# adaLN transformer block: chunk 0's high parts straight from the transposes, the first query weights split on GpSimd

## The chip, the core and the metric

The kernel runs on one core of a Trainium2 chip. The engines of a core run side by side, each through its own queue in order: TensorE (PE, and PEld for its weight loads), VectorE (DVE), ScalarE (ACT), GpSimd (POOL) and SyncE (SP, which issues most DMAs). They wait for each other through semaphores. The metric is the time of one execution in microseconds (us), as the median of several runs.

## The reference

One transformer block whose two layer norms are modulated by a condition `c`; 2048 rows of 512 values, 32 heads of 16, a hidden width of 1792, all in float32.

```python
mod = (_silu(c) @ w_mod).reshape(c.shape[0], 6, 1, -1)
sa, ca, ga, sb, cb, gb = (mod[:, 0], mod[:, 1], mod[:, 2], mod[:, 3], mod[:, 4], mod[:, 5])
h = _layernorm(x, axis=-1) * (1 + ca) + sa
x = x + ga * _A_ref(h, A_wqkv, A_wo)      # qkv projection, softmax attention, output projection
h = _layernorm(x, axis=-1) * (1 + cb) + sb
x = x + gb * _B_ref(h, B_w_gate, B_w_up, B_w_down)   # (silu(h @ w_gate) * (h @ w_up)) @ w_down
```

## The kernel before

The rows are worked on in four chunks of 512. Matrix products run in a split form: an operand is written as a high part (rounded to the type fp32r) and a low part (the value less its high part), and a product takes three matmuls: high by high, high by low, low by high. So every operand needs two results: `hT[0]` and `hT[1]` for the modulated, transposed rows of a chunk, `wqs[0]` and `wqs[1]` for the weights of the projections.

The order on each engine is the order in which the code is written out (a manual schedule). A tile framework puts in the semaphore waits, tile by tile.

The change lies in the start-up, before the projections of chunk 0 run without a pause. There the following happens, in this order:

- SP loads the rows `xt`, then for each half `ab` of the 512 features the condition's weights `wm_ab` and, behind each, 128 columns of the projection weights: the first 128 key columns (`wst0[:, 0]`) and the first 128 query columns (`wst0[:, 1]`).
- VectorE computes the statistics of the rows (`stats`) and normalizes them (`norm`, tiles `nt`).
- `mod_part` multiplies the condition by half of `w_mod` on TensorE (L286) into PSUM bank 7 and copies the result to `ev` on ScalarE (L289). `mod_col` turns `ev` on TensorE (L295), sums the pieces on VectorE (`cs`, L297) and writes the columns `modc` of scale and bias (L300).
- `turn` transposes the normalized rows on TensorE (L165), one PSUM bank for each of the four blocks k of 128 features (`tps0`, banks 0 to 3).
- `half_prep(ab)` modulates the two blocks k = 2ab and 2ab+1 into the float32 tile `h32`: the first on VectorE (L172), the second, with `fast`, on ScalarE (L170). ScalarE then rounds each `h32` to its high part (L350), and VectorE subtracts for the low part (L353). The first call stands before the projections, the second behind the third of their matmuls.
- The key columns are split by `split_w`: the high part by ScalarE (L205), the low part by GpSimd (L206). The query columns: the high part by ScalarE (L360), the low part by VectorE (L353), at the head of the subtractions of `half_prep(1)`.

The first job of the projections is `both` of key block 0 and query block 0. Its 24 matmuls (L213) stand in an order by halves of the features: six of the key job for k = 0 and 1 (high by high, low weights, low rows), six of the query job for k = 0 and 1 (high by high, low rows, low weights), then the same two groups of six for k = 2 and 3. The other projections follow without a gap. The transposes of chunk 0 and all that comes later (the other chunks, scores and softmax, the feed-forward layers) are not touched by the change.

Of the kernel before, what the change touches and what calls it, by code (L numbers as in the profile page):

```python
# [11 lines left out]
F32 = mybir.dt.float32  # L12
F32R = mybir.dt.float32r
BF = mybir.dt.bfloat16
I32 = mybir.dt.int32
AF = mybir.ActivationFunctionType
ALU = mybir.AluOpType
# [4 lines left out]
P = 128  # L22
# [6 lines left out]
NK = D // P  # L29
NC = 4  # L30
CW = S // NC
# [25 lines left out]
def run(it):  # L57
    for _ in it:
        pass
# [44 lines left out]
def block_kernel(ctx, tc, x, wqkv, wo, w_gate, w_up, w_down, c, w_mod, out):  # L104
    nc = tc.nc
# [18 lines left out]
    four, bank, single = Turn(0, 1, 2, 3), Turn(4, 5, 6), Turn(7)  # L124
# [18 lines left out]
    def stats(pool, xt, keep):  # L143
        st = pool.tile([P, 4, 6], F32, name="stt", tag="stt", bufs=2)
        mv = pool.tile([P, 4, 2], F32, name="mv", tag="mv", bufs=2)
        rs = pool.tile([P, 4], F32, name="rs", tag="rs", bufs=2)
        for i in range(4):
            nc.vector.bn_stats(st[:, i, :], xt[:, i, :])
            nc.vector.bn_aggr(mv[:, i, :], st[:, i, :])
            yield  # L150
        nc.scalar.activation(rs, mv[:, :, 1], AF.Sqrt, bias=eps_t[:, 0:1])
        keep += [mv, rs]
# [10 lines left out]
    def turn(tp, rows, k):  # L163
        for i, nt in enumerate(rows):
            nc.tensor.transpose(tp[:, i * P:(i + 1) * P], nt[:, k * P:(k + 1) * P], ident)  # L165

    def modulate(pool, hT, tp, vec, k, fast=False, copy=True):
        h32 = pool.tile([P, CW], F32, name="h32", tag="h32", bufs=2)
        if fast:
            nc.scalar.activation(h32, tp, AF.Identity, scale=modc[:, vec, k:k + 1], bias=modc[:, vec + 1, k:k + 1])  # L170
        else:
            nc.vector.tensor_scalar(h32, tp, modc[:, vec, k:k + 1], modc[:, vec + 1, k:k + 1],  # L172
                                    op0=ALU.mult, op1=ALU.add)
        if copy:
            nc.scalar.copy(hT[0][:, k, :], h32)
        return hT[1][:, k, :], h32, hT[0][:, k, :].bitcast(F32)

    def prep(pool, xt, hT, vec, lat):
# [76 lines left out]
    wm_ab = []  # L255
# [27 lines left out]
    def mod_part(wm, copy=nc.scalar.copy):  # L283
        pb_ = single("pmod")
        for k in range(NK):
            nc.tensor.matmul(pb_[32 * k:32 * k + 32, :], sc[:, k:k + 1].to_broadcast([P, 32]), wm[:, k, :],  # L286
                             start=True, stop=True)
        ev = pa.tile([P, D], F32, name="ev", tag="ev", bufs=1)
        copy(ev, pb_)  # L289
        return ev  # L290
# [28 lines left out]
    def split_w(src, c0, eng=nc.gpsimd):  # L319
        cols = slice(c0, c0 + P)  # L320
        split(wqs[0][:, :, cols], wqs[1][:, :, cols], src, eng)
# [4 lines left out]
    hT = {0: new_hT()}  # L326
    keep0 = []
    run(stats(pa, xt[0], keep0))
    split_w(wst0[:, 0], D)
    ev = mod_part(wm_ab[0])  # L330
    rows0 = list(norm(pa, xt[0], keep0))

    def half_cols(ab):
# [1 line left out]

    tps0 = []

    def turn_two(k):
        for e in range(2):
            tps0.append(four("tp"))  # L340
            turn(tps0[-1], rows0, k + e)

    def half_prep(ab, ev, extra=None):
        mod_col(ev, half_cols(ab))
        if ab == 0:
            turn_two(2)
        tps = tps0[2 * ab:2 * ab + 2]
        lows = [modulate(pa, hT[0], tps[e], 0, 2 * ab + e, e, False) for e in range(2)]
        for _, h32, high in lows:
            nc.scalar.copy(high.bitcast(F32R), h32)  # L350
        nxt = mod_part(wm_ab[1]) if ab == 0 else None
        for low in ([extra] if extra else []) + lows:
            nc.vector.tensor_sub(*low)  # L353
        return nxt

    bank = Turn(4, 5, 6, 7)
    turn_two(0)
    ev = half_prep(0, ev)
    wq0 = [w[:, :, 0:P] for w in wqs]
    nc.scalar.copy(wq0[0], wst0[:, 1])  # L360

    def weights():
        st_ = {}
# [94 lines left out]
    for ci in range(NC - 1):  # L458
        jobs = [proj_T(ci, w, m, 1 if ci or m else 2) for w, m in kq[:6 if ci == NC - 2 else 8]]
        if ci < NC - 2:  # L460
            jobs += [proj_v(4 * ci + t) for t in range(4)]
        hT[ci + 1] = new_hT()
        if ci == 0:
            jobs[0:2] = [both(*jobs[0:2], 6)]
        if ci == 1:
            bank = Turn(4, 5, 6)
            sm.add("m", 7, mods())
        if ci:
            sm.add("p", 5 if ci < NC - 2 else 3, prep(pa, xt[ci + 1], hT[ci + 1], 0, 1))
        for i, _ in enumerate(sm.jobs(jobs)):  # L470
            if ci == 0 and i == 2:
                half_prep(1, ev, (wq0[1], wst0[:, 1], wq0[0].bitcast(F32)))
            if ci == 0 and i == 5:
                take(weights_, 2)
                sm.add("w", 5, weights_)
            if ci == 0 and i == 24:
                sm.add("p", 5, prep(pa, xt[1], hT[1], 0, 1))
            if i == 40:
                load_k0(ci)
            if i == 44 and ci + 2 < NC:  # L480
                load_x(ci + 2)
        while sm.lanes["p"][1]:
            run(sm.lanes["p"][1].pop(0))
# [706 lines left out]
```

## Time and profile before

| | us |
|---|---|
| median of 3 runs | 1826.32 (1826.1 to 1827.04) |
| the profiled execution | 1826.86 |
| its span (first to last instruction) | 1825.0 |
| busy: PE / PEld / DVE / ACT / POOL | 1816.3 / 1202.5 / 1521.2 / 1248.0 / 459.9 |

The span is what the trace covers; the profiled execution's own time is 1.86 us longer. TensorE is busy nearly all of the span, at the full granted clock. A busy TensorE is not one at its peak, since its matmuls are pipelined: it shows as busy also where another engine sets its pace. What sets the end is read from the chain of waits, followed back from the last instruction.

### The profile page before, as it was taken

The numbers are of one execution on the slowest core, as the hardware profiler recorded it, in microseconds if no ns is written. First come the engines' busy times: TensorE is split into PE (matmuls) and PEld (weight loads), VectorE is DVE, ScalarE is ACT, GpSimd is POOL, SyncE is SP. The second block draws the span as 40 slices with busy tenths as digits, with TensorE's granted clock in tenths as the row PEclk, the third lists the DMA queues.
The fourth block names the chain that finished last, engine by engine and source line by source line (L and its number), as shares of the span: only waits on it lengthen the run. The fifth ranks groups of instructions, "written<-read, shape, count | busy, mean of one in ns | idle before, by whom it ended". The sixth has DMA issues, their size and how long they took to land.

```text
span 1825.0 us, 40961 instructions
## 1 busy us (share of the span) xinstructions
PE 1816.3 (100%) x16904; PEld 1202.5 (66%) x16904; DVE 1521.2 (83%) x2554; ACT 1248.0 (68%) x2358; POOL 459.9 (25%) x538
## 2 busy tenths in 40 slices
PE   9999999999999999999999999999999999999999
PEld 7876444444465777776565777776564577777887
DVE  5578999999999888888999888889999988832544
ACT  4223888888888766777888767767888876673211
POOL 3612544556223111111123111111113011131200
PEclk9999999999999999999999999999999999999999
DMA  9883876667845444453544554444643536333742
GB/s 307 288 232 138 203 199 172 179 167 199 207 81 125 103 122 143 115 149 70 145 110 105 141 125 118 122 118 91 161 80 57 116 90 157 134 123 120 279 167 108
DMA packets 80486, 267.62 MB, mean 147 GB/s; under 512 B 19604, under 2 KB 24212, under 8 KB 59620
## 3 DMA queue, kind: packets, MB, share of 16 engines
q1 hardware_dynamic: 61324, 179.71, 34.0%
q0 software_dynamic: 18288, 84.49, 19.5%
q8 instruction: 133, 2.18, 0.5%
q10 hardware_dynamic: 688, 0.80, 0.1%
q14 instruction: 53, 0.43, 0.1%
HBM read 201.85 MB, written 62.13 MB: 145 GB/s over the span
## 4 chain that ended last, share of the span: by engine, by line
PE 83%; DVE 14%; ACT 1%; DMA 0%; issue 0%; SPq 0%; DVEq 0%
PE bank L586 21%; PE bank L789 20%; PE bank L571 14%; DVE mx L525 14%; PE bank L523 11%; PE bank L808 8%; PE bank L213 7%; PE bank L851 1%; PE bank L772 0%; DMA wm_ab<-in_w_mod 0%; PE bank L165 0%; ACT sq L832 0%; DVE v_flat L882 0%; PE bank L537 0%; SPq L261 0%
## 5 line engine op out<-in xcount | busy, mean ns | idle before, releaser
L525 DVE TENSOR_REDUCE mx<-bank 128x1 f32<-128x512 f32 x2048 | 1273.3, 681 | 111.0 <-PE bank L523 63.7
L571 PE MATMUL bank<-qop,kop 50*128 50x512 f32 x2048 | 729.7, 426 | 0.4 <-ACT pt__16494 L573 0.2
L523 PE MATMUL bank<-kop,qop 48*128 48x512 f32 x2048 | 724.6, 425 | 0.3
L571 PEld LDWEIGHTS bank<-qop,kop 50*128 50x128 f32 x2048 | 343.1, 184 | 168.9 <-issue 49.8
L523 PEld LDWEIGHTS bank<-kop,qop 48*128 48x128 f32 x2048 | 342.8, 184 | 106.2 <-DVE mx L525 62.1
L789 PE MATMUL bank<-act,wgu 64*128 64x512 f32 x1872 | 303.5, 392 | 0.0
L789 PEld LDWEIGHTS bank<-act,wgu 64*128 64x128 f32 x1872 | 199.4, 187 | 22.5
L613 POOL TENSOR_TENSOR on<-o,rb 128x512 f32<-128x512 f32 x31 | 39.9, 1286 | 507.8 <-DMA rb<-d_dr 359.0
L789 PE MATMUL bank<-wd,mid 64*128 64x512 f32 x912 | 131.6, 391 | 0.0
L870 POOL CAST mid<-m 128x512 fp32r<-128x512 f32 x40 | 24.4, 609 | 380.5 <-DVE m L868 273.7
L789 PEld LDWEIGHTS bank<-wd,mid 64*128 64x128 f32 x912 | 92.2, 186 | 11.2
L213 PE MATMUL bank<-hT,wqs 128*128 128x512 f32 x384 | 94.4, 397 | 0.4 <-DVE wqs L353 0.4
L866 DVE SCALAR_TENSOR_TENSOR q<-th,bank 128x512 f32<-128x512 f32 x56 | 38.3, 683 | 54.2 <-ACT th L862 54.2
L213 PEld LDWEIGHTS bank<-hT,wqs 128*128 128x128 f32 x384 | 70.6, 188 | 19.1 <-issue 3.2
L862 ACT ACTIVATE th<-bank 128x512 f32<-128x512 f32 x56 | 33.2, 594 | 57.9 <-PE bank L808 57.9
L882 DVE TENSOR_TENSOR x<-bank,x 128x512 f32<-128x512 f32 x84 | 53.9, 685 | 16.1 <-PE bank L789 16.1
L868 DVE TENSOR_TENSOR m<-bank,q 128x512 f32<-128x512 f32 x56 | 38.7, 692 | 21.7 <-PE bank L808 19.7
L871 POOL TENSOR_TENSOR mid<-m,mid 128x512 fp32r<-128x512 f32 x40 | 51.7, 1292 | 3.3
L808 PE MATMUL bank<-wd,mid 128*128 128x512 f32 x216 | 51.3, 393 | 0.0
L213 PE MATMUL bank<-wqs,hT 128*128 128x512 f32 x192 | 48.0, 398 | 0.0
L789 PE MATMUL bank<-wgu,act 64*128 64x512 f32 x288 | 47.6, 392 | 0.0
L808 PEld LDWEIGHTS bank<-wd,mid 128*128 128x128 f32 x216 | 40.4, 188 | 8.9
(6300 smaller groups left out, 5137.3 us busy)
## 6 DMA issues: line engine op xcount, KB each, us to landing
wgu<-gu_dr SPq DMA_DIRECT2D x48, 1024.0 KB
wd<-wd_dr SPq DMA_DIRECT2D x28, 1024.0 KB
kop<-kd SPq DMA_DIRECT2D x33, 768.0 KB
kop<-kd POOLq DMA_DIRECT2D x29, 768.0 KB, 8.8
gu_dr<-wgu POOLq DMA_DIRECT2D x14, 1024.0 KB, 13.6
kd<-prt SPq DMA_DIRECT2D x16, 512.0 KB
qd<-prt SPq DMA_DIRECT2D x16, 512.0 KB
kop<-gu_dr SPq DMA_DIRECT2D x8, 1024.0 KB
```

The source lines that it names most:

```text
L213: nc.tensor.matmul(pt, lhs(a, k), rhs(b, k), start=(n == 0), stop=(n == 3 * nk - 1))
L523: nc.tensor.matmul(pm, qop[u][rows, s, qt * P:(qt + 1) * P], kop[u % 3][rows, s, kc * CW:(kc + 1) * CW], start=True, stop=True)
L525: nc.vector.tensor_reduce(mx[u][:, b, s, qt, kc:kc + 1], pm, op=ALU.max, axis=AX.X)
L571: nc.tensor.matmul(sp, kop[u % 3][rows, h // 2, kt * P:(kt + 1) * P], qop[u][rows, h // 2, :], start=True, stop=True)
L586: nc.tensor.matmul(pv[u][32 * h:32 * h + 32, cols], v_flat[:, e0:e0 + 32], p_[h][:, cols], start=(kt == 0 and half == 0), stop=(kt == 15), ...
L613: mul.tensor_mul(on, o, rb)
L789: mm = nc.tensor.matmul(outs[e], lhs(e, a, k)[rows], rhs(b, k)[rows], start=(ph == 0 and j == 0), stop=(j == z and (ph == 1 or trade)), sk ...
L808: nc.tensor.matmul(outs[e], lhs(e, a, k), rhs(b, k), start=(j == 0), stop=(j == z))
L866: nc.vector.scalar_tensor_tensor(q, th, 1.0, outs[0], op0=ALU.add, op1=ALU.mult)
L868: nc.vector.tensor_mul(m32, outs[1], q)
L871: (nc.gpsimd if slow else nc.vector).tensor_sub(mid[:, 1, :], m32, mid[:, 0, :].bitcast(F32))
L882: nc.vector.tensor_add(ch.x2[:, t, :], outs[e], ch.x2[:, t, :])
```

## The change

- `half_prep` no longer calls `modulate` (which loses its options `fast` and `copy`). For each block k ScalarE computes the modulated rows from the transposes' bank directly into the high part `hT[0]`, and VectorE computes the same from the same bank into `h32`; then VectorE subtracts for the low part.
- The first query columns are split on GpSimd: it rounds the high part and subtracts for the low part. ScalarE's cast and VectorE's subtraction for them go.
- The copy of the first `ev` stands before the cast of the first key columns on ScalarE.
- Only one block of rows is transposed before `ev` is turned, the other three behind it.

```diff
     run(stats(pa, xt[0], keep0))
+    ev = mod_part(wm_ab[0])
     split_w(wst0[:, 0], D)
-    ev = mod_part(wm_ab[0])
...
-    def half_prep(ab, ev, extra=None):
+    def turn_next():
+        tps0.append(four("tp"))
+        turn(tps0[-1], rows0, len(tps0) - 1)
+
+    def half_prep(ab, ev):
         mod_col(ev, half_cols(ab))
-        if ab == 0:
-            turn_two(2)
-        tps = tps0[2 * ab:2 * ab + 2]
-        lows = [modulate(pa, hT[0], tps[e], 0, 2 * ab + e, e, False) for e in range(2)]
-        for _, h32, high in lows:
-            nc.scalar.copy(high.bitcast(F32R), h32)
+        while len(tps0) < NK:
+            turn_next()
+        lows = []
+        for k in (2 * ab, 2 * ab + 1):
+            scale, bias = modc[:, 0, k:k + 1], modc[:, 1, k:k + 1]
+            h32 = pa.tile([P, CW], F32, name="h32", tag="h32", bufs=2)
+            nc.scalar.activation(hT[0][0][:, k, :], tps0[k], AF.Identity, scale=scale, bias=bias)
+            nc.vector.tensor_scalar(h32, tps0[k], scale, bias, op0=ALU.mult, op1=ALU.add)
+            lows.append((hT[0][1][:, k, :], h32, hT[0][0][:, k, :].bitcast(F32)))
         nxt = mod_part(wm_ab[1]) if ab == 0 else None
-        for low in ([extra] if extra else []) + lows:
+        for low in lows:
             nc.vector.tensor_sub(*low)
         return nxt
...
-    turn_two(0)
+    turn_next()
     ev = half_prep(0, ev)
     wq0 = [w[:, :, 0:P] for w in wqs]
-    nc.scalar.copy(wq0[0], wst0[:, 1])
+    nc.gpsimd.tensor_copy(wq0[0], wst0[:, 1])
+    nc.gpsimd.tensor_sub(wq0[1], wst0[:, 1], wq0[0].bitcast(F32))
...
-                half_prep(1, ev, (wq0[1], wst0[:, 1], wq0[0].bitcast(F32)))
+                half_prep(1, ev)
```

VectorE's queue from the first sum of the condition's columns to the last low part of chunk 0, with the engine whose semaphore each row waits for. First the kernel before (`h_204` and `h_242` are VectorE's blocks 0 and 2; banks 63 to 66 are banks 0 to 3, bank 70 is bank 7):

```order
L297 TENSOR_REDUCE cs<-bank_67 128x4 [waits PE_49]
L300 TENSOR_SCALAR modc<-cs 128x2 [waits DVE_49]
L300 TENSOR_SCALAR modc<-cs 128x2
L172 TENSOR_SCALAR h_204<-bank_63,modc 128x512 [waits DVE_49]
L353 TENSOR_TENSOR hT_150<-h_204,hT_149 128x512 [waits Activation_49]
L353 TENSOR_TENSOR hT_150<-h_206,hT_149 128x512 [waits Activation_49]
L297 TENSOR_REDUCE cs<-bank_70 128x4 [waits PE_49,Activation_49]
L300 TENSOR_SCALAR modc<-cs 128x2 [waits DVE_49]
L300 TENSOR_SCALAR modc<-cs 128x2
L172 TENSOR_SCALAR h_242<-bank_65,modc 128x512 [waits DVE_49]
L353 TENSOR_TENSOR wqs_116<-wq_106,wqs_115 128x4x128 [waits DMAHW2_49,Activation_49]
L353 TENSOR_TENSOR hT_150<-h_242,hT_149 128x512 [waits Activation_49]
```

The same place in VectorE's queue in the changed kernel, from the first modulation on:

```order
L347 TENSOR_SCALAR h_204<-bank_63,modc 128x512 [waits Activation_49]
L347 TENSOR_SCALAR h_207<-bank_64,modc 128x512 [waits Activation_49]
L351 TENSOR_TENSOR hT_150<-h_204,hT_149 128x512 [waits DVE_49]
L351 TENSOR_TENSOR hT_150<-h_207,hT_149 128x512 [waits DVE_49]
L293 TENSOR_REDUCE cs<-bank_70 128x4 [waits PE_49,Activation_49]
L296 TENSOR_SCALAR modc<-cs 128x2 [waits DVE_49]
L296 TENSOR_SCALAR modc<-cs 128x2
L347 TENSOR_SCALAR h_243<-bank_65,modc 128x512 [waits Activation_49]
L347 TENSOR_SCALAR h_246<-bank_66,modc 128x512 [waits Activation_49]
L351 TENSOR_TENSOR hT_150<-h_243,hT_149 128x512 [waits DVE_49]
```

VectorE now modulates two blocks in each half instead of one, each behind a wait for ScalarE; the subtraction for the query weights is gone, and the low parts wait for VectorE itself.

ScalarE's queue between the square root of the statistics and the casts of the later weights, before:

```order
L205 CAST wqs_115<-wq_106 128x4x128 [waits DMAHW7_49]
L289 COPY ev<-bank_70 128x512 [waits PE_49]
L170 ACTIVATE h_206<-bank_64,modc 128x512 [waits DVE_49,PE_49]
L350 CAST hT_149<-h_204 128x512 [waits DVE_49]
L350 CAST hT_149<-h_206 128x512 [waits Activation_49]
L289 COPY ev<-bank_70 128x512 [waits PE_49]
L360 CAST wqs_115<-wq_106 128x4x128 [waits DMAHW2_49]
L170 ACTIVATE h_244<-bank_66,modc 128x512 [waits DVE_49,Activation_49]
L350 CAST hT_149<-h_242 128x512 [waits DVE_49]
L350 CAST hT_149<-h_244 128x512 [waits Activation_49]
```

And in the changed kernel:

```order
L285 COPY ev<-bank_70 128x512 [waits PE_49]
L201 CAST wqs_115<-wq_106 128x4x128 [waits DMAHW7_49]
L346 ACTIVATE hT_149<-bank_63,modc 128x512 [waits DVE_49,PE_49]
L346 ACTIVATE hT_149<-bank_64,modc 128x512 [waits PE_49]
L285 COPY ev<-bank_70 128x512 [waits PE_49,Activation_49]
L346 ACTIVATE hT_149<-bank_65,modc 128x512 [waits DVE_49]
L346 ACTIVATE hT_149<-bank_66,modc 128x512
```

ScalarE writes all four high parts itself from banks 0 to 3, and three instructions are gone from its queue.

## Rows read from the trace of the kernel before

**Rows 1.** The page: span, granted clock in 40 slices, chain by engine.

```profile
span 1825.0 us, 40961 instructions
...
PEclk9999999999999999999999999999999999999999
...
PE 83%; DVE 14%; ACT 1%; DMA 0%; issue 0%; SPq 0%; DVEq 0%
```

**Rows 2.** The chain's pieces at the start: start us, us, what.

```profile
5.94 8.71 DMA wm_ab<-in_w_mod
...
17.84 0.69 issue
18.53 0.69 DVE wqs L353
...
19.27 17.34 PE bank L213 x75
```

**Rows 3.** PE's timeline, 9 to 36: start us, us, engine, line, what, [idle before].

```profile
10.87 1.06 PE L286 MATMUL bank<-wm_ab,sc 128*32 128x512 f32 x8 [0.63 <-DMA wm_ab<-in_w_mod]
...
14.79 1.07 PE L286 MATMUL bank<-wm_ab,sc 128*32 128x512 f32 x8 [0.45 <-DMA wm_ab<-in_w_mod]
15.78 0.96 PE L213 MATMUL bank<-hT,wqs 128*128 128x512 f32 x3
16.58 0.62 PE L295 MATMUL bank<-ident,ev 128*128 128x128 f32 x4
16.96 1.87 PE L213 MATMUL bank<-hT,wqs 128*128 128x512 f32 x7
```

**Rows 4.** ACT's timeline, 11.6 to 20.6.

```profile
11.65 0.62 ACT L205 CAST wqs<-wq 128x512 fp32r<-128x512 f32 x1 [2.72 <-DMA wq<-in_A_wqkv]
12.17 0.58 ACT L289 COPY ev<-bank 128x512 f32<-128x512 f32 x1
14.04 0.78 ACT L170 ACTIVATE h<-bank,modc 128x512 f32<-128x512 f32 x1 [1.29 <-DVE modc L300]
14.83 1.14 ACT L350 CAST hT<-h 128x512 fp32r<-128x512 f32 x2
15.91 0.59 ACT L289 COPY ev<-bank 128x512 f32<-128x512 f32 x1
16.39 0.62 ACT L360 CAST wqs<-wq 128x512 fp32r<-128x512 f32 x1
17.86 0.78 ACT L170 ACTIVATE h<-bank,modc 128x512 f32<-128x512 f32 x1 [0.85 <-DVE modc L300]
18.65 1.14 ACT L350 CAST hT<-h 128x512 fp32r<-128x512 f32 x2
```

**Rows 5.** DVE's timeline, 13.95 to 20.6.

```profile
15.48 1.29 DVE L353 TENSOR_TENSOR hT<-h,hT 128x512 fp32r<-128x512 f32 x2 [0.69 <-ACT hT L350]
17.32 0.18 DVE L297 TENSOR_REDUCE cs<-bank 128x4 f32<-128x16 f32 x1 [0.55 <-PE bank L295]
17.53 0.24 DVE L300 TENSOR_SCALAR modc<-cs 128x2 f32<-128x2 f32 x2
17.81 0.81 DVE L172 TENSOR_SCALAR h<-bank,modc 128x512 f32<-128x512 f32 x1
...
19.30 1.29 DVE L353 TENSOR_TENSOR hT<-h,hT 128x512 fp32r<-128x512 f32 x2
```

**Rows 6.** POOL's timeline, 10 to 34.

```profile
20.39 12.68 POOL L206 TENSOR_TENSOR wqs<-wq,wqs 128x512 fp32r<-128x512 f32 x10 [6.76 <-ACT wqs L205]
```

**Rows 7.** Line L407, a cast of the same size on POOL: ns min/median/max, first and last start.

```profile
L407 POOL CAST prt<-prt x9: 611/612/615, 114.4 to 162.2; 128x512 fp32r<-128x512 f32 x9
```

**Rows 8.** Line L774, the modulation of the second layer norm on ACT.

```profile
L774 ACT ACTIVATE h<-bank,modc x16: 770/793/833, 573.5 to 1701.4; 128x512 f32<-128x512 f32 x16
```

**Rows 9.** PE's waits from 20 to the end: us in total, times, longest.

```profile
PE bank L772 <- DVE mx L525: 0.6, 3, 0.2
```

**Rows 10.** SP's timeline, 11 to 28.

```profile
19.28 0.37 SPq L368 DMA_DIRECT2D wq<-in_A_wqkv  x1
```

More of the change, by code (lines that the diff above doesn't have):

```diff
@@ L165, in turn, with modulate @@
             nc.tensor.transpose(tp[:, i * P:(i + 1) * P], nt[:, k * P:(k + 1) * P], ident)
-    def modulate(pool, hT, tp, vec, k, fast=False, copy=True):
+    def modulate(pool, hT, tp, vec, k):
         h32 = pool.tile([P, CW], F32, name="h32", tag="h32", bufs=2)
[L169 to L175, printed above, removed]
+        nc.vector.tensor_scalar(h32, tp, modc[:, vec, k:k + 1], modc[:, vec + 1, k:k + 1],
+                                op0=ALU.mult, op1=ALU.add)
+        nc.scalar.copy(hT[0][:, k, :], h32)
         return hT[1][:, k, :], h32, hT[0][:, k, :].bitcast(F32)
@@ L336, in block_kernel @@
     tps0 = []
[L338 to L341, printed above, removed]
-    def half_prep(ab, ev, extra=None):
-        mod_col(ev, half_cols(ab))
-        if ab == 0:
-            turn_two(2)
-        tps = tps0[2 * ab:2 * ab + 2]
-        lows = [modulate(pa, hT[0], tps[e], 0, 2 * ab + e, e, False) for e in range(2)]
-        for _, h32, high in lows:
-            nc.scalar.copy(high.bitcast(F32R), h32)
+    def turn_next():
+        tps0.append(four("tp"))
+        turn(tps0[-1], rows0, len(tps0) - 1)
+    def half_prep(ab, ev):
+        mod_col(ev, half_cols(ab))
+        while len(tps0) < NK:
[7 more added lines that the diff above has]
+            lows.append((hT[0][1][:, k, :], h32, hT[0][0][:, k, :].bitcast(F32)))
         nxt = mod_part(wm_ab[1]) if ab == 0 else None
-        for low in ([extra] if extra else []) + lows:
+        for low in lows:
             nc.vector.tensor_sub(*low)
```

## The prediction

> **What bounds the kernel now.** First the page: TensorE is busy over the whole span at the full granted clock, and the chain that ended last runs 83% on TensorE and 14% on VectorE, with DMA at 0% in the rounding [rows 1]. So a delay of TensorE at the start should travel to the end. I then read the list of TensorE's waits after 20 us: the longest group is 0.6 us in three waits, and none is for a DMA [rows 9]. There is little later on in which a delay or a gain could be lost.
>
> The chain at the start shows the place: the second half of the condition's weights lands at 14.65, and from 19.27 on 75 matmuls follow without a gap [rows 2]. What the change can move is the stretch between these two. There TensorE multiplies the condition (14.79 to 15.86), runs three matmuls of the first key block, turns `ev`, runs seven more until 18.83 (16.96 + 1.87) [rows 3], and then waits until VectorE has the low part of the query weights at 19.21 (18.53 + 0.68) [rows 2]. The reader should see why this is late: VectorE modulates block 2 from 17.81 [rows 5] and only then subtracts for the weights, though ScalarE had their high part at 17.01 [rows 4].
>
> The gap costs more than its idle time. Matmuls in a row start 0.23 us apart (17.34 over 75, rows 2). The first step behind a break is longer: three matmuls take 0.96 [rows 3], that is steps of 0.34 and 0.23 and a last matmul of 0.39; the seven in 1.87 have a first step of 0.32 in the same way. Without the wait the eighth would so start at 18.67 (16.96 + 0.32 + 6 x 0.23); it starts at 19.27. That is 0.60, and 0.11 more for the longer step behind it.
>
> **What is removed.** The wait for the query weights goes. GpSimd takes cast and subtraction: 0.61 [rows 7] and 1.27 (12.68 over 10, rows 6). ScalarE could cast these columns at 16.39 without waiting for their DMA [rows 4], so they have landed by then, and GpSimd, whose subtraction for the key columns ends about 14.5 (ScalarE's cast behind `ev` at 13.1, then 1.3), has the high part by 17.00 and the low part by 18.3 at the latest. TensorE wants the high part at its fourth of the seven, 17.74, and the low part at the eighth, 18.67. So this costs nothing. Behind it in GpSimd's queue stand the later weights' subtractions, from 20.39 on [rows 6]; they lose nothing either. SP's load of the value weights, issued at 19.28 [rows 10] behind that subtraction, can go some 1 to 2 us earlier; nothing on TensorE's path waits for it in this stretch.
>
> The `ev` copy of the first half no longer stands behind a cast: TensorE's product ends at 11.93 [rows 3], and by the 0.05 from TensorE to ScalarE seen at 15.86 to 15.91 [rows 3, 4] the copy starts at 11.98 instead of 12.17. Turn, sum and columns follow 0.17 to 0.19 earlier. This gains nothing at the end, since the product of the second half waits for its landing at 14.65 in any case; the three blocks transposed later on TensorE end at about 14.6, just ahead of it.
>
> **What is added.** The listing of VectorE's queue in the section on the change carries the step that decides. Both engines now read the same bank for each block, and each of VectorE's modulations waits for ScalarE: block k is read by ScalarE first, and only then by VectorE. In the kernel before, VectorE starts its block 2 at 17.81 and ScalarE its block 3 at 17.86, side by side on two banks [rows 4, 5].
>
> The Trainium skill, "PSUM — Partial Sum Buffer", section "PSUM bank collisions raise a hardware error", says that two engines that are in one bank at once raise an error and read wrong data, "ScalarE-read with VectorE-read included". By that rule the waits in the listing are needed and the two modulations can't be one beside the other; without it the sum would be the gain of the first rival below. No row of this trace has two engines in one bank at once, so the trace neither bears it out nor speaks against it.
>
> So VectorE has twice the modulations, each behind ScalarE's. First half: columns 0.17 earlier, ScalarE 13.87 to 14.65 and 14.56 to 15.34 (0.78 each, rows 4; an instruction starts some 0.09 before the end of the one ahead), VectorE 14.69 to 15.50 and 15.41 to 16.22 (0.81, rows 5), low parts until 17.42 (1.29 for two, rows 5). TensorE wants the second of them at 17.51: in time. But the sum of the second half on VectorE starts at about 17.35 instead of 17.32, and the columns are there at 17.80 instead of 17.77.
>
> Second half: ScalarE 17.89 to 18.67 and 18.58 to 19.36. VectorE 0.03 behind each: 18.70 to 19.51 and 19.42 to 20.23. Low parts 20.14 to 20.83 and 20.74 to 21.43. Before, they ended at 19.99 and 20.59 (19.30 + 1.29). Here lies the price: 0.84 us on the last low part.
>
> **The sum.** TensorE after: eighth matmul 18.67, ninth 18.90, tenth 19.13 (its high part at 18.67), eleventh 19.42 (waits for 19.36), thirteenth at 19.9, then it waits for the low parts: fourteenth 20.89, fifteenth 21.49, and the sixteenth, behind a break, 21.83. Before: eighth 19.27, ninth 19.61, sixteenth 21.23. So the end of the start-up comes 0.60 us later: the removed wait gives 0.71, the new ones take 1.31.
>
> Bounds. A modulation that writes the high part's type from a bank isn't in the trace. Its nearest rows are a plain copy out of a bank, 0.58 [rows 4], and the same operation with float32 out, 0.77 to 0.83 [rows 8]. With 0.59 the fifteenth starts at 21.30 and the loss is 0.41; with 0.83 it is 0.65. I take 0.78, as the operation is the same and only the type written differs. A gain out of this one term could come only without the wait; that is a rival.
>
> The profiled execution took 1826.86, its span 1825.0; it stands 0.54 above the median of the runs. The sum makes it 1827.46, and the median 1826.32 + 0.60 = **1826.9**.
>
> **The rivals.**
>
> No price for the shared bank (gain of 0.3): if VectorE's modulations ran beside ScalarE's, block 2 would end at 18.65, block 3 at 19.37, the low parts at 19.97 and 20.57, TensorE's fifteenth would start at 20.63 and the sixteenth at 20.97, 0.26 ahead of before: 1826.0. For it speaks that removing the wait is right on TensorE's side; against it the waits in the listing. This is also the case in which the parts that the change is made of do what they look like.
>
> Absorbed: the delay is lost on the way, because the pace is set by VectorE or a load for long stretches (14% of the chain is VectorE's, rows 1), or because the early load of the value weights helps: 1826.3. Against it: VectorE's work there is itself released by TensorE, so a delay shifts both, and rows 9 show no wait for a load.
>
> Slower by over 0.2%: the granted clock. Between 20 and 21.4 TensorE would start one matmul, after a start-up full of breaks. If the grant fell there from 2.4 to 1.2 GHz, each matmul behind would take 0.23 more. It decides from some 13 matmuls on (3.65 less 0.6, over 0.23); with 16 the time is 1826.9 + 3.7 = 1830.6. Against it: the clock shows full in every slice [rows 1], and waits of 0.63 and 0.45 at 10.9 and 14.8 [rows 3] did not change it.
>
> **How the numbers follow.** The two modulations one after the other 0.70; absorbed 0.13; no price 0.11; the clock 0.04; something that wins over 0.2%, which I can't name, 0.02. About 0.2% (3.65 us) is what a measurement of this kernel can tell from no change: all but the last two cases lie within, so same 0.94, slower 0.04, faster 0.02. The range: at the low end the no-price case on the lowest run (1826.1 - 0.3 = 1825.8), at the high end the upper bound on the highest (1827.04 + 0.65 = 1827.7); runs on another day may lie a third of the spread of 0.94 outside on either side, so 1825.5 to 1828.0.
>
> **What would show it.** Right: VectorE's modulations of blocks 2 and 3 start at about 18.7 and 19.4, each with ScalarE as its releaser; the gap before the eighth matmul (released by VectorE's weights) is gone, and a new one of some 0.7 us at 20.1 to 20.9 stands before the fourteenth, with a second at 21.3, released by VectorE's low parts; GpSimd's cast and subtraction end by 18.3. Wrong: VectorE's modulations beside ScalarE's in time; a wait of TensorE for GpSimd; a clock below full after 21; or TensorE's run without gaps starting before 21.2.

## The result, and the profile after

| | before | after |
|---|---|---|
| median | 1827.04 us of 7 runs (1826.1 to 1828.79) | 1833.0 us of 7 runs (1831.8 to 1835.83) |
| ratio of the times | | 1.0032, 95% interval 1.0021 to 1.0044 |
| the profiled execution, its span | 1826.86, 1825.0 | 1835.83, 1833.9 |

The change makes the kernel about 6 us slower, 0.32%. 1826.9 was predicted, with 1828.0 as the upper end. A loss was predicted, but only a tenth of this one.

The page of the changed kernel, against [rows 1]: the granted clock in 40 slices and the chain by engine.

```profile
PEclk9999999999999999999999999999999999999999
...
PE 88%; DVE 8%; DMA 2%; ACT 1%; SPq 0%; issue 0%; DVEq 0%; ACTq 0%
```

A loss of 0.3% doesn't show here. One slice is 46 us wide, so a clock that is halved for 3 us rounds away in it. The chain's pieces tell more (start us, us, what; against [rows 2]):

```profile
21.25 3.20 DVE hT L351 x2
24.49 17.07 PE bank L209 x68
```

The last thing that TensorE waits for in the start-up is no longer the query weights but VectorE's two last low parts, 3.20 us of the path. They took 1.29 in [rows 5]. The run without gaps starts at 24.49.

VectorE's timeline of the changed kernel, 9 to 34 (start us, us, engine, line, what, count, idle before), against [rows 5]:

```profile
13.46 1.02 DVE L296 TENSOR_SCALAR modc<-cs 128x2 f32<-128x2 f32 x2
15.40 1.53 DVE L347 TENSOR_SCALAR h<-bank,modc 128x512 f32<-128x512 f32 x2 [0.91 <-ACT hT L346]
16.84 1.67 DVE L351 TENSOR_TENSOR hT<-h,hT 128x512 fp32r<-128x512 f32 x2
...
18.63 0.24 DVE L296 TENSOR_SCALAR modc<-cs 128x2 f32<-128x2 f32 x2
19.72 1.53 DVE L347 TENSOR_SCALAR h<-bank,modc 128x512 f32<-128x512 f32 x2 [0.85 <-ACT hT L346]
21.16 3.27 DVE L351 TENSOR_TENSOR hT<-h,hT 128x512 fp32r<-128x512 f32 x2
```

GpSimd's timeline of the same stretch, against [rows 6]:

```profile
13.11 1.28 POOL L202 TENSOR_TENSOR wqs<-wq,wqs 128x512 fp32r<-128x512 f32 x1 [9.72 <-ACT wqs L201]
15.39 0.61 POOL L358 CAST wqs<-wq 128x512 fp32r<-128x512 f32 x1 [0.99 <-DMA wq<-in_A_wqkv]
16.08 1.28 POOL L359 TENSOR_TENSOR wqs<-wq,wqs 128x512 fp32r<-128x512 f32 x1
20.94 13.41 POOL L202 TENSOR_TENSOR wqs<-wq,wqs 128x512 fp32r<-128x512 f32 x10 [3.57 <-ACT wqs L201]
```

Read the two side by side. Where one of GpSimd's subtractions runs, VectorE's subtractions of two SBUF tiles, and its columns from SBUF to SBUF, are long: the first columns 1.02 beside the subtraction of 13.11, but 0.24 at 18.63 when GpSimd is idle; the low parts 1.67 beside that of 16.08, and 3.27 beside those from 20.94 on. The modulations, which read a bank, keep their 0.8 each throughout, those at 16.1 beside GpSimd too. GpSimd is held as well: its ten subtractions take 13.41 instead of the 12.68 of [rows 6]. But not everything in SBUF is long. The statistics of the next chunk's rows also go from SBUF to SBUF, beside the same ten subtractions, and take the 0.66 to 0.69 that they take alone:

```profile
28.93 0.68 DVE L148 BATCH_NORM_STATS2 stt<-xt 128x6 f32<-128x512 f32 x1
```

TensorE's timeline, 9 to 45, against [rows 3]:

```profile
14.68 1.06 PE L282 MATMUL bank<-wm_ab,sc 128*32 128x512 f32 x8 [0.16 <-DMA wm_ab<-in_w_mod]
...
17.97 3.41 PE L209 MATMUL bank<-hT,wqs 128*128 128x512 f32 x12 [0.48 <-DVE hT L351]
22.81 0.49 PE L209 MATMUL bank<-hT,wqs 128*128 128x512 f32 x1 [1.44 <-DVE hT L351]
24.49 17.07 PE L209 MATMUL bank<-hT,wqs 128*128 128x512 f32 x68 [1.18 <-DVE hT L351]
41.40 1.03 PE L165 MATMUL bank<-ident,nt 128*128 128x128 f32 x8
```

The wait for the query weights is gone. Three waits for low parts stand in its place, 0.48, 1.44 and 1.18. I measure the start-up from the start of the condition's second product (here 14.68) to the next chunk's first transposes (here 41.40): 26.72. The timeline of the kernel before goes on behind [rows 3] with

```profile
19.27 17.34 PE L213 MATMUL bank<-hT,wqs 128*128 128x512 f32 x75 [0.43 <-DVE wqs L353]
36.45 1.03 PE L165 MATMUL bank<-ident,nt 128*128 128x128 f32 x8
```

So it has 36.45 - 14.79 = 21.66 for the same work, and 21.81 in a second profile. So 5.0 us are lost here. Of these, 1.4 are in the 68 matmuls, which take 17.07 where 15.7 is full pace (below). They lie in the granted clock; busy time in each stretch (PE, PEld, DVE, ACT, POOL, then the granted clock, DMA share, GB/s):

```profile
22.00:24.00 2.00, 0.49 (x1) 0.19 (x1) 2.00 (x2) 0.94 (x2) 2.00 (x3) 0.98 1.04 390
24.00:26.00 2.00, 1.51 (x4) 1.22 (x5) 0.50 (x2) 0.68 (x2) 2.00 (x2) 0.50 0.71 258
26.00:28.00 2.00, 2.00 (x8) 1.57 (x7) 0.63 (x1) 0.72 (x2) 2.00 (x2) 0.67 0.30 107
...
207.00:216.00 9.00, 8.56 (x63) 3.99 (x63) 5.35 (x10) 4.53 (x10) 0.00 (x0) 0.62 0.41 167
```

After two microseconds in which TensorE ran one matmul the grant is 0.50, that is 1.2 GHz, and from 28 on it is full again. In this execution it fell a second time, at 208, behind a wait of 1.3 us for a transfer (`qop<-qd`). The span is 8.9 longer here: 5.0 from the start-up, the rest from that place. A second profile of the changed kernel (below) has neither fall.

### The profile page after: what moved, and what is told of

Same layout as the page of the kernel before. It is cut to its first block, busy times and chain, and to the rows that moved or that the text cites. A ratio compares the mean times of both kernels' runs of the same rounds, so it can differ in the third digit from the quotient of the medians.

```text
span 1833.9 us, 40959 instructions
## 1 busy us (share of the span) xinstructions
PE 1821.4 (99%) x16904; PEld 1203.2 (66%) x16904; DVE 1523.2 (83%) x2555; ACT 1246.6 (68%) x2355; POOL 461.0 (25%) x540
## 4 chain that ended last, share of the span: by engine, by line
PE 88%; DVE 8%; DMA 2%; ACT 1%; SPq 0%; issue 0%; DVEq 0%; ACTq 0%
PE bank L585 23%; PE bank L788 20%; PE bank L570 15%; PE bank L522 13%; PE bank L807 8%; DVE mx L524 7%; PE bank L209 7%; DMA qop<-qd 1%; PE bank L850 1%; PE bank L771 0%; DMA wm_ab<-in_w_mod 0%; PE bank L165 0%; DVE hT L351 0%; ACT sq L831 0%; PE bank L536 0%
## 5 line engine op out<-in xcount | busy, mean ns | idle before, releaser
L788 PEld LDWEIGHTS bank<-wd,mid 64*128 64x128 f32 x912 | 91.7, 186 | 11.5
L881 DVE TENSOR_TENSOR x<-bank,x 128x512 f32<-128x512 f32 x84 | 53.8, 684 | 16.1 <-PE bank L788 16.1
L867 DVE TENSOR_TENSOR m<-bank,q 128x512 f32<-128x512 f32 x56 | 38.7, 691 | 21.7 <-PE bank L807 19.7
```

Of the source, the lines that this page charges most:

```text
L788: mm = nc.tensor.matmul(outs[e], lhs(e, a, k)[rows], rhs(b, k)[rows], start=(ph == 0 and j == 0), stop=(j == z and (ph == 1 or trade)), sk ...
L867: nc.vector.tensor_mul(m32, outs[1], q)
L881: nc.vector.tensor_add(ch.x2[:, t, :], outs[e], ch.x2[:, t, :])
```

## The experiments

Two theories stood after this. The one called SERIAL was the prediction's own: the price lies in VectorE's modulations that wait for ScalarE on the shared bank. The one called PORT: a VectorE instruction whose operands all lie in SBUF and an instruction of GpSimd can't run at the same time, so the split on GpSimd lengthens VectorE's work. A third question was what the clock adds. The ratios in the table are taken over all runs of both kernels, and so are not exactly the quotients of the two medians beside them.

| kernel | median, us | before beside it | ratio | start-up stretch in its profile, us |
|---|---|---|---|---|
| before | | | | 21.66, 21.81 |
| after | 1833.0 | 1827.04 | 1.0032 [1.0021, 1.0044] | 26.72, 25.35 |
| e1_hold | 1829.11 | 1827.14 | 1.0009 [1.0, 1.0019] | 23.44 |
| e2_banks_apart | 1828.35 | 1827.14 | 1.0006 [0.9997, 1.0016] | 22.72 |
| e3_query_only | 1828.08 | 1827.14 | 1.0009 [1.0, 1.0018] | 22.18 |
| e4_shared_only | 1831.9 | 1827.14 | 1.0029 [1.0019, 1.004] | 25.90 |
| e5_fill | 1831.28 | 1826.85 | 1.0023 [1.0014, 1.0033] | 25.42 |
| e6_serial | 1828.23 | 1826.85 | 1.001 [1.0001, 1.0019] | 22.34 |
| e7_in_bank | 1828.79 | 1826.85 | 1.0009 [1.0, 1.0018] | 22.98 |
| e9_immune | 1827.82 | 1827.16 | 1.0002 [0.9993, 1.0012] | 21.63 |

**GpSimd held back until the last low part is done** (e1_hold). One tiny copy that reads that low part stands ahead of GpSimd's later subtractions; all else is the changed kernel.

```diff
             if ci == 0 and i == 5:
+                nc.gpsimd.tensor_copy(pa.tile([P, 1], F32, name="held"), hT[0][1][:, 3, CW - 1:CW].bitcast(F32))
                 take(weights_, 2)
```

> The changed kernel, with GpSimd's subtractions for the later weights held back until VectorE's last low part of chunk 0 is written (a one-column copy on GpSimd that reads it). Theory PORT: a GpSimd subtraction in SBUF and a VectorE subtraction whose operands both lie in SBUF exclude each other; in the changed kernel VectorE's last two low parts took 3.27 us, each ending 0.55 after a GpSimd subtraction ended, and before 1.29. Then here the two take 1.29 again (21.16 to 22.45), TensorE's fifteenth matmul starts at about 22.5 instead of 24.49, its waits are under 1 us each, the granted clock stays full, and the time is 1 to 2.5 us over the kernel before, that is 3 to 5 us under the changed one. Rival SERIAL: only the waits for ScalarE and the order of VectorE's queue matter; then the two low parts still take over 2.5 us and the time stays with the changed kernel's, within 1 us.

Its timeline (VectorE, GpSimd, TensorE):

```profile
21.04 1.28 DVE L351 TENSOR_TENSOR hT<-h,hT 128x512 fp32r<-128x512 f32 x2
...
22.39 0.19 POOL L473 COPY held<-hT 128x1 f32<-128x1 f32 x1 [5.15 <-DVE hT L351]
22.53 12.61 POOL L202 TENSOR_TENSOR wqs<-wq,wqs 128x512 fp32r<-128x512 f32 x10
...
21.77 16.32 PE L209 MATMUL bank<-hT,wqs 128*128 128x512 f32 x69 [0.52 <-DVE hT L351]
```

The two low parts take 1.28 instead of 3.27, TensorE's waits of 1.44 and 1.18 shrink to one of 0.52, and two thirds of the loss are gone, though every modulation still waits for ScalarE. GpSimd isn't held either: its ten take 12.61, and end only 0.8 later (35.14 against 34.35). At this place PORT is borne out, and SERIAL can't be the large part.

**Modulations on two banks again, split on GpSimd** (e2_banks_apart).

```diff
-        for k in (2 * ab, 2 * ab + 1):
+        for e, k in enumerate((2 * ab, 2 * ab + 1)):
...
-            nc.scalar.activation(hT[0][0][:, k, :], tps0[k], AF.Identity, scale=scale, bias=bias)
-            nc.vector.tensor_scalar(h32, tps0[k], scale, bias, op0=ALU.mult, op1=ALU.add)
+            if e:
+                nc.scalar.activation(h32, tps0[k], AF.Identity, scale=scale, bias=bias)
+            else:
+                nc.vector.tensor_scalar(h32, tps0[k], scale, bias, op0=ALU.mult, op1=ALU.add)
...
+        for _, h32, high in lows:
+            nc.scalar.copy(high.bitcast(F32R), h32)
```

> The changed kernel with the modulations as before: one block of each pair on VectorE, the other on ScalarE, from two banks, and the high parts as casts on ScalarE; the rest of the change stays (query weights on GpSimd, order of the first copies and transposes). PORT: VectorE's columns of the first half still take about 1.0 (beside GpSimd's key subtraction, 13.1 to 14.4) and one of the first two low parts is held by the query subtraction (16.1 to 17.4), so the second half's columns come at 18.4 to 18.9 as in the changed kernel; but the last two low parts end at 21.0 to 21.9, mostly ahead of GpSimd's next subtraction: TensorE's fifteenth matmul at 21.5 to 22, and a time 0.3 to 1.5 us over the kernel before. SERIAL: with no shared bank nothing is left that is slower, so the time is at the kernel before's or up to 0.5 us under it, and the columns of the second half come at 17.6 to 17.8.

Its timeline:

```profile
16.49 2.38 DVE L355 TENSOR_TENSOR hT<-h,hT 128x512 fp32r<-128x512 f32 x2 [0.69 <-ACT hT L352]
...
20.77 1.29 DVE L355 TENSOR_TENSOR hT<-h,hT 128x512 fp32r<-128x512 f32 x2 [0.69 <-ACT hT L352]
```

The meetings of the first half are all there (low parts 2.38, the columns 1.01), but the last low parts start before GpSimd's later subtractions (21.85 here) and take 1.29. What is left of the loss is not told apart from nothing by the median; the stretch says +1.0.

**The query split on GpSimd alone, in the kernel before** (e3_query_only).

```diff
-    nc.scalar.copy(wq0[0], wst0[:, 1])
+    nc.gpsimd.tensor_copy(wq0[0], wst0[:, 1])
+    nc.gpsimd.tensor_sub(wq0[1], wst0[:, 1], wq0[0].bitcast(F32))
...
-                half_prep(1, ev, (wq0[1], wst0[:, 1], wq0[0].bitcast(F32)))
+                half_prep(1, ev)
```

> The kernel before with one part of the change alone: the first query columns are split on GpSimd. PORT: GpSimd's query subtraction (about 16.1 to 17.4) holds up VectorE's second low part of the first half by up to 0.8, the columns of the second half come up to 0.6 later, and TensorE's wait at 18.84 goes: fifteenth matmul between 20.7 and 21.4 (before 21.01), time within 0.5 us of the kernel before. SERIAL: VectorE's low parts keep their places (15.48 and 16.09), so the fifteenth matmul starts at 20.4 to 20.7 and the time is 0.3 to 0.6 under the kernel before.

Its timeline:

```profile
14.94 1.71 DVE L353 TENSOR_TENSOR hT<-h,hT 128x512 fp32r<-128x512 f32 x2 [0.69 <-ACT hT L350]
17.00 0.90 DVE L300 TENSOR_SCALAR modc<-cs 128x2 f32<-128x2 f32 x2
...
16.18 1.62 POOL L361 TENSOR_TENSOR wqs<-wq,wqs 128x512 fp32r<-128x512 f32 x1
...
19.45 14.88 PE L213 MATMUL bank<-hT,wqs 128*128 128x512 f32 x63 [0.70 <-ACT hT L350]
```

The part of the change that was to win 0.71 wins nothing (the stretch is 0.4 longer): TensorE's wait for the query weights is gone, and one of 0.70 for the high parts replaces it, since the columns that these need took 0.90 beside GpSimd. The columns of the first half keep their 0.24 here (13.17): the copy of `ev` stands behind the key columns' cast as before, so GpSimd's key subtraction is over at 13.08.

**The shared bank alone, in the kernel before** (e4_shared_only): the changed `half_prep`, and the query weights split as before.

```diff
-        lows = [modulate(pa, hT[0], tps[e], 0, 2 * ab + e, e, False) for e in range(2)]
-        for _, h32, high in lows:
-            nc.scalar.copy(high.bitcast(F32R), h32)
+        lows = []
+        for k in (2 * ab, 2 * ab + 1):
...
+            nc.scalar.activation(hT[0][0][:, k, :], tps0[k], AF.Identity, scale=scale, bias=bias)
+            nc.vector.tensor_scalar(h32, tps0[k], scale, bias, op0=ALU.mult, op1=ALU.add)
```

> The kernel before with the other part of the change alone: in each half ScalarE writes the high parts from the transposes' banks and VectorE modulates the same two banks behind it; the query weights stay on ScalarE and VectorE. PORT: in the second half VectorE has three subtractions from about 20.3 on, and GpSimd's subtractions for the later weights start at about 20.1; each of VectorE's then waits for one of GpSimd's, they end at 21.9, 23.7 and 25.5, TensorE waits for each, the clock falls as in the changed kernel, and the time is 5 to 7.5 us over the kernel before, no less than the changed kernel's. SERIAL: VectorE's three end at 21.0, 21.7 and 22.3, the fifteenth matmul starts at 22.4 and the time is 1 to 2 us over the kernel before.

Its timeline:

```profile
23.56 1.58 DVE L357 TENSOR_TENSOR wqs<-wq,wqs 128x512 fp32r<-128x512 f32 x1
25.07 3.44 DVE L357 TENSOR_TENSOR hT<-h,hT 128x512 fp32r<-128x512 f32 x2
...
25.20 19.08 PE L213 MATMUL bank<-hT,wqs 128*128 128x512 f32 x75 [2.87 <-DVE wqs L357]
```

One part without the other loses nearly as much as both, 1.0029. The two modulations in a row (22.12 to 23.65) make VectorE late; being late, its three subtractions meet GpSimd's, which began at 23.34, and take 5.0 instead of 2.0 [rows 2, 5]. TensorE's wait for the query weights, 0.43 in the kernel before, is 2.87. So SERIAL and PORT aren't two prices to be added: the first brings the second about. (In this profile the condition's weights landed late and the clock was halved twice; the stretch of 25.90 leaves out the first of these, and holds the second: its 75 matmuls take 19.08 instead of 17.34.)

**Spare matmuls in the two waits** (e5_fill): work for TensorE that delays nothing, to hold the clock up.

```diff
+            if ci == 0 and i in (15, 16):
+                for _ in range(6):
+                    nc.tensor.matmul(banks[4], wqs[0][:, 0, D:D + P], hT[0][0][:, 0, :], start=True, stop=True)
```

> The changed kernel with twelve spare matmuls (into a bank that nobody reads) for TensorE to do while it waits: six ahead of the first key block's low rows of block 2, six ahead of those of block 3, where it waited 1.44 and 1.18 us. Theory CLOCK: of the changed kernel's loss 1.4 us come because the granted clock falls to half from 23.9 to 27.3 behind these waits. Then here the clock stays at 1.00 through 20 to 30 us, VectorE's low parts end as late as in the changed kernel (24.4), TensorE's gapless run starts at 24.5 and reaches the next transposes 15.6 later instead of 17.1, and the time is 0.8 to 2 us under the changed kernel's, 3 to 4.5 over the kernel before. Rival: the clock falls with the phase of something else, not for the waits; then it falls here too and the time stays with the changed kernel's.

Its timeline of TensorE (L474 is the spare work):

```profile
21.20 1.55 PE L474 MATMUL bank<-hT,wqs 128*128 128x512 f32 x6
...
24.55 15.69 PE L209 MATMUL bank<-hT,wqs 128*128 128x512 f32 x68
```

The granted clock is full in every stretch from 22 to 28, and the 68 matmuls behind take 15.69 instead of 17.07. The low parts still take 3.32. The mean clock is below 1.0 in 1 of its 10 runs and in 3 of the 25 of the kernel before beside it; in the changed kernel it is in 5 of 7. The median is 1.7 us lower than that of the changed kernel, and its ratio 1.0023 against 1.0032. So the clock's part is some 1.4 us by the stretch of one profile with the fall and some 1.6 by the ratios, though the intervals of the two overlap.

**The serial modulations with no meeting at all** (e6_serial). It leaves out the low part of the first query columns (zeros stand in its place).

```diff
+    nc.gpsimd.memset(wqs[1][:, :, 0:P].bitcast(F32), 0.0)
...
-    ev = mod_part(wm_ab[0])
     split_w(wst0[:, 0], D)
+    ev = mod_part(wm_ab[0])
...
-    nc.gpsimd.tensor_sub(wq0[1], wst0[:, 1], wq0[0].bitcast(F32))
...
+                nc.gpsimd.tensor_copy(pa.tile([P, 1], F32, name="held"), hT[0][1][:, 3, CW - 1:CW].bitcast(F32))
```

> The changed kernel with every meeting of GpSimd and VectorE in SBUF taken away, so that the waits between ScalarE and VectorE on the shared banks are left alone: the first key columns are cast ahead of the copy of ev again, GpSimd's later subtractions are held until the last low part, and the low part of the first query columns is left out (zeros, written at the start). This is what the prediction priced at 0.60. If that price is right, VectorE's first columns take 0.24, the low parts 1.29 for two in both halves, and the fifteenth matmul starts 21.3 to 21.8 after the start (the landing of the condition's second half at about 14.65; later if that is later), time 0.3 to 1.2 us over the kernel before. If the serial modulations cost more by themselves, for instance because a bank is read more slowly behind the other engine, the low parts end past 22.

Its timeline:

```profile
13.42 0.24 DVE L297 TENSOR_SCALAR modc<-cs 128x2 f32<-128x2 f32 x2
...
19.95 1.28 DVE L352 TENSOR_TENSOR hT<-h,hT 128x512 fp32r<-128x512 f32 x2
...
20.69 13.57 PE L209 MATMUL bank<-hT,wqs 128*128 128x512 f32 x57 [0.53 <-DVE hT L352]
```

Apart from that low part, this is the kernel that the prediction described: every VectorE instruction has the duration that it had before, and the stretch is 0.6 longer (22.34 against 21.66 and 21.81); 0.60 was predicted. The medians say +1.4; the ratio's interval is 0.2 to 3.5 us.

**The modulated rows written back to their bank** (e7_in_bank): the changed kernel, whose low parts now read PSUM.

```diff
-            h32 = pa.tile([P, CW], F32, name="h32", tag="h32", bufs=2)
+            h32 = tps0[k]
```

> The changed kernel with VectorE's modulated rows written back into their own bank instead of SBUF, so that the low part's subtraction has one operand in PSUM and one in SBUF. Nothing else is changed, GpSimd does what it does. PORT: only instructions with all operands in SBUF are held, so the two low parts of each half take 1.3 to 1.45 even though GpSimd's subtractions run at the same time; the columns of the first half still take 1.0; the second columns come 0.3 to 0.5 earlier than in the changed kernel, the fifteenth matmul starts at 22 to 22.5, the clock stays full, time 0.8 to 2.2 us over the kernel before. Rival: GpSimd's work holds up VectorE whatever it reads (writes to SBUF, queue, semaphores); then the last two low parts still take 3.3 and the time is the changed kernel's.

Its timeline:

```profile
16.15 1.28 DVE L351 TENSOR_TENSOR hT<-bank,hT 128x512 fp32r<-128x512 f32 x2
...
20.07 1.27 DVE L351 TENSOR_TENSOR hT<-bank,hT 128x512 fp32r<-128x512 f32 x2
...
15.43 1.28 POOL L359 TENSOR_TENSOR wqs<-wq,wqs 128x512 fp32r<-128x512 f32 x1
19.85 12.77 POOL L202 TENSOR_TENSOR wqs<-wq,wqs 128x512 fp32r<-128x512 f32 x10 [3.13 <-ACT wqs L201]
```

Here nothing is moved away from GpSimd: both low pairs run beside its subtractions, and take 1.28 and 1.27. For these subtractions one operand in PSUM is enough. The columns, still from SBUF to SBUF, are held as before (1.02). This is the cleanest sign for PORT: the same engines, about the same distance in time (GpSimd's begin 0.72 and 0.22 ahead of VectorE's, in the changed kernel 0.76 and 0.22), the same amount of work, another place of one operand. As worded above PORT is too wide, though: the statistics go from SBUF to SBUF and aren't held.

**A version without the serial step and without a meeting** (e9_immune): on the kernel before, the query split on GpSimd, the column sums in a bank, the rows modulated in their bank, and ScalarE writing the second block's high part directly (`rows_in_bank(k)` is VectorE's modulation of block k, written back to its own bank; the query split is that of e3_query_only).

```diff
-        cs = pa.tile([P, NK], F32, name="cs", tag="cs", bufs=2)
+        cs = pc_[:, 1:1 + NK]
...
+        rows_in_bank(a)
+        nc.scalar.activation(hT[0][0][:, b, :], tps0[b], AF.Identity, scale=modc[:, 0, b:b + 1],
+                             bias=modc[:, 1, b:b + 1])
+        nc.scalar.copy(hT[0][0][:, a, :], tps0[a])
+        rows_in_bank(b)
+        lows = [(hT[0][1][:, k, :], tps0[k], hT[0][0][:, k, :].bitcast(F32)) for k in (a, b)]
...
```

> A try at a version ahead of both: the query weights on GpSimd as in the change, but no VectorE instruction with all operands in SBUF while GpSimd works. In each half VectorE modulates one block in its own bank and ScalarE takes the other block's high part straight from its bank and casts the first block's from the bank; then VectorE modulates the second block in its bank; the low parts and the columns' sums are read from PSUM. PORT: VectorE's columns take 0.24 in both halves and the low parts 1.3 for two, though GpSimd's query subtraction lies beside them; TensorE's wait for the query weights is gone and at most 0.6 us of waits for high parts are left; from the start of the condition's second product to the transposes of the next chunk it takes 21.2 to 21.6 us (kernel before 21.66 and 21.81, changed kernel 26.7). The time would be 0.2 to 0.5 us under the kernel before, which lies inside what the comparison can tell (same). Rival: writing into PSUM or reading it twice costs more; then the stretch takes over 21.9 us.

Its timeline of VectorE:

```profile
15.70 0.23 DVE L300 TENSOR_SCALAR modc<-bank 128x2 f32<-128x2 f32 x2
...
17.56 1.28 DVE L361 TENSOR_TENSOR hT<-bank,hT 128x512 fp32r<-128x512 f32 x2
```

No instruction of VectorE is held, and TensorE runs from 18.61 without a wait. Yet the time is that of the kernel before, 1.0002 [0.9993, 1.0012]. Its stretch is 21.63, just above the 21.2 to 21.6 that was expected, but its profile is a poor one for that (the clock was halved from 11.5 to 14.9), so whether some tenths were won stays open. No version here beats the kernel before.

**Both kernels once more** (e8_before_again, e10_after_again), one profile each, for what is chance in a single one.

> The kernel before once more, for a second profile of it: what of the differences at about 200 us (the wait for the query rows' load, 1.3 us in the changed kernel's profile and none in the first profile of the kernel before) comes and goes with the same kernel. If it is chance, this profile may show 0 to 1.3 there; if it belongs to the change, it shows none. The start should repeat: low parts at 19.3 and 19.9 relative to a landing at 14.65, clock full.

> The changed kernel once more, for a second profile: the start should repeat (columns of the first half 1.0 us, the last two low parts 3.2 to 3.4, waits of TensorE of about 1.4 and 1.2, 25.4 to 26.9 us from the condition's second product to the next transposes). The second loss of its first profile, 3.9 us at 207 to 215 us (a wait of 1.3 us for the query rows' load, then half clock for 6.8 us), belongs to the change if it is there again, and to chance if it isn't; the clock after the start may or may not fall, as its phase differs from execution to execution.

The kernel before repeats itself: 1827.53, stretch 21.81, and no wait for the query rows' load (`qop<-qd`). The changed kernel took 1830.46; its timeline:

```profile
21.67 3.27 DVE L351 TENSOR_TENSOR hT<-h,hT 128x512 fp32r<-128x512 f32 x2
...
23.33 0.51 PE L209 MATMUL bank<-hT,wqs 128*128 128x512 f32 x1 [1.42 <-DVE hT L351]
25.00 15.71 PE L209 MATMUL bank<-hT,wqs 128*128 128x512 f32 x68 [1.17 <-DVE hT L351]
```

Its busy time and granted clock by stretch, columns as above:

```profile
24.00:26.00 2.00, 0.99 (x4) 0.86 (x5) 0.95 (x1) 0.46 (x1) 2.00 (x2) 1.00 0.97 357
...
207.00:216.00 9.00, 9.00 (x98) 4.48 (x96) 8.91 (x16) 7.60 (x16) 0.69 (x2) 1.00 0.22 89
```

The same 3.27 and, to 0.02, the same two long waits; but the clock stays full, and there is no loss at 208. The wait at 208 so comes and goes with the same changed kernel; the two profiles of the kernel before, both without it, don't tell whether the change makes it more likely. The held low parts belong to the kernel, the fall of the clock to the execution.

## Why the prediction was wrong

**Where the time went**, by the stretches of the table, against 21.7 before:

| term | us | from |
|---|---|---|
| serial modulations, less the removed wait | +0.6 | e6_serial |
| first half: columns held 0.78, low parts 0.38 longer (0.31 in the second profile) | +1.1 | e1_hold less e6_serial |
| last two low parts beside GpSimd's later subtractions | +1.9 | after (second profile) less e1_hold |
| clock at 1.2 GHz for about 3 us, in some executions | +1.4 | after, first profile less second |

That is 3.65 without a fall of the clock and 5.0 with one, before rounding. The ratio's interval is 3.8 to 8.0 us. What the medians have beyond the stretches, some 0.3 to 0.8 us in e1_hold, e6_serial and e7_in_bank and 1.0 to 2.3 in the changed kernel, stays open; later waits for transfers such as that of 1.3 at 208 are in some profiles (1.2 in e1_hold, 0.4 in e6_serial, 0.5 in e7_in_bank) and not in others (none in the second of the changed kernel), so part of it may be chance.

**What was right.** The step on the shared bank: VectorE's two last modulations end 2.38 behind the second columns (18.87 to 21.25), 2.43 was predicted, and e6_serial shows its price by itself. ScalarE's 0.78 for a high part from a bank holds: two take 1.45. GpSimd has the query weights at 17.36, before the 18.3 given. SP's load of the value weights is issued at 17.39 instead of 19.28 [rows 10], and nobody gains by it.

**The step that failed** is the overlap of VectorE with GpSimd, put at nothing in "So this costs nothing". I asked whether GpSimd's results come in time for TensorE, and whether anybody stands behind it in its queue. I did not ask who else works while it works. Every duration of VectorE in my sum came from [rows 5], where GpSimd is idle until 20.39, and was then laid beside a running GpSimd. Three places show it:

- "Turn, sum and columns follow 0.17 to 0.19 earlier". The copy of `ev` now stands ahead of the key columns' cast, so GpSimd's key subtraction runs later (13.11 to 14.39) and lies on the columns, which are held 0.78. In the kernel before the two just miss each other: the subtraction is over at 13.63 and the columns start at 13.71 (its trace). This part of the change was not run by itself; with the old order, in e3_query_only and e6_serial, these columns take 0.24.
- "low parts until 17.42 (1.29 for two, rows 5)". The query subtraction on GpSimd makes them 0.38 longer.
- "Low parts 20.14 to 20.83 and 20.74 to 21.43". [rows 6] has GpSimd's later subtractions from 20.39 on: the meeting stood in the prediction's numbers. They take 3.27. In the kernel before VectorE's last low part was already under way, 19.91 to 20.59, when GpSimd began; the change doesn't touch those subtractions, but its delay brings VectorE among them (the low parts start 6.48 behind the condition's second product, before 4.51), and that costs 1.9 more.

Together that is 3.0 us for a term that the sum had at nothing; it is the larger part of the loss, and where the clock falls, that fall comes behind the waits that it lengthens.

And the trace of before did hold a row that shows the price, later in the program, where I took no term from. The line of the normalization (ns min/median/max):

```profile
L159 DVE TENSOR_SCALAR nt<-xt,mv,rs x16: 529/544/1807, 9.2 to 94.7; 128x512 f32<-128x512 f32 x16
```

Its instruction for the next chunk and GpSimd's last subtraction, from the timeline of before:

```profile
32.03 1.32 DVE L159 TENSOR_SCALAR nt<-xt,mv,rs 128x512 f32<-128x512 f32 x1
...
31.76 1.32 POOL L206 TENSOR_TENSOR wqs<-wq,wqs 128x512 fp32r<-128x512 f32 x1
```

The same instruction from SBUF to SBUF takes 0.53 alone and 1.32 here, and ends 0.27 behind GpSimd's (33.35 and 33.08). A maximum three times the median in a line whose shapes are all alike is a question that should have been asked.

The Trainium skill states the rule: "SBUF — State Buffer", section "Who interferes with whom", says that VectorE and GpSimd share one pair of ports, and that a VectorE instruction with two inputs in SBUF contends with a GpSimd instruction that reads SBUF. By the same section of the Trainium skill, one with at most one input in SBUF contends only in a mode that takes both ports, which `tensor_scalar` can enter; there the one that issues first keeps the shared pair for its whole instruction. The traces agree: the low parts with both inputs in SBUF are held (3.27), with one in PSUM they are not (1.27); the first columns, a `tensor_scalar` behind a subtraction of 13.11 to 14.39, end at 14.42; the statistics, with one input, are not held (0.68). Which mode an instruction ran in, no trace shows. I had read it as a matter of GpSimd's speed only and cited the skill for the bank alone.

**The clock.** This rival had 4%, because waits of 0.63 and 0.45 had not changed the clock [rows 1, 3]. It came in part. But the waits of the changed kernel are not the 0.7 and the shorter one behind it that I worked out, they are 1.44 and 1.18 with one matmul between, more than twice those that I held as evidence. So the chance hung on the size of another term, the one that failed. The price was too high: 3.7 for sixteen matmuls at half clock, where 1.4 was seen, some six at 0.23.

**The other rivals.** "No price for the shared bank" is refuted: in every profile with the shared bank VectorE's modulation follows ScalarE's on the same bank. "Absorbed" is refuted as well: e10_after_again's span is 3.6 longer than that of before, its stretch 3.65. Whether the waits on the shared bank are needed was not tried.

## What to carry to other kernels

Before work is moved to GpSimd, list what VectorE runs in the same microseconds: in this kernel its subtractions of two SBUF tiles, its normalization and its columns from SBUF to SBUF were held until GpSimd's subtraction was done, and GpSimd in turn, while the statistics and whatever read a bank were not. Moving an instruction on another engine can bring about such a meeting too, as the earlier copy of `ev` did. Leave one operand in PSUM where the value comes from there anyway, or put GpSimd's work behind VectorE's by a true dependence. And take a duration from a row whose neighbours on the other engines are those that it will have after the change.

## What was not expected of the hardware

- A VectorE subtraction of two 128x512 tiles in SBUF takes 0.68 us alone and 1.59 to 1.75 beside GpSimd's subtractions (its trace); two of them 3.27 instead of 1.29. One with a PSUM operand isn't touched (1.27 for two beside GpSimd). A pair of `tensor_scalar` of 128x2 in SBUF is held too: 1.02 instead of 0.24. The statistics of 128x512 from SBUF are not: 0.66 to 0.69 beside GpSimd and alone.
- GpSimd is held as well: ten subtractions 13.41 instead of 12.68, one 1.62 (e3_query_only) and 1.78 (e2_banks_apart) instead of 1.28.
- With the same program and the same two waits of 1.4 and 1.2 us, the granted clock fell to a half (0.50) in one profile and stayed full (1.00) in another. A single profile doesn't tell the price of such a wait.
